# Scaling the hidden values in PSUM, eight plain products in two of twelve groups, and a longer spacing of the weight narrowing, in a fused attention, mixture and feed-forward kernel

## The chip, the cores and the metric

One Trainium2 chip, one core of it. The metric is the device time of one execution in microseconds (us). Three runs of the kernel before gave a median of 903.39 us (902.93 to 903.54).

## What is computed

Three stages in a row, all in fp32 (the last stage's weights arrive as 64-bit floats and are narrowed to fp32 on the chip):

```python
q_pool = q.reshape(B, H, S // 2, 2, D).mean(axis=3)          # B 2, H 8, S 1152, D 64
attn = softmax(q_pool @ k.T / sqrt(D)); x = attn @ v          # x: 1152 tokens x 512
p = domain_probs / domain_probs.sum(-1)                       # 1152 x 4
for e in range(4):                                            # w1: 4 x 512 x 1024
    out += p[:, e:e+1] * (maximum(x @ w1[e], 0) @ w2[e])
h = out @ w_in                                                # 512 x 2048
y = where(h > 0, h, exp(minimum(h, 0)) - 1) @ w_out           # 2048 x 512
```

## The kernel before

**Stages and groups.** `attention_then_moe_then_elu_ffn` runs attention first (16 heads), then twelve groups that are built alike: groups 0 to 7 are the mixture (4 experts, two groups of 512 hidden columns each), groups 8 to 11 the feed-forward part (G1 is 8). All activations stay transposed: `acc` holds x, later the output, as 128 partitions x 4 chunks x 1152 tokens.

**One group.** A group has a first product (512 features to 512 hidden) and a second (512 hidden to 512 features). Every fp32 matrix is split into a high and a low part (`h` and `l` in the names), and a product is three matmuls: high by high, low by high, high by low (`product`, L1086). The first product is done with seven block products in place of eight (a Strassen scheme): `TURNS` lists the seven, each needs a sum or difference of quarters of the weights (`left_sum`, then `left_high` and `left_low`, tiles `sum`, `wh`, `wl`) and of quarters of x (`x_half_sum` and `x_half_high`, `x_half_low`, tiles `XH`, `XL`, `K`, `xh`, `xl`, `x4h`, `x4l`; the sums of x are written over `acc`). Each block product is done for two halves s of its 576 tokens; one such unit ("F") is 12 matmuls of 288 columns, so a group has 14 F units. Between units, partial sums leave PSUM: `keep` (ScalarE copies, tiles `u` and `c`) and `whole` (VectorE adds a PSUM bank and a kept sum, result in an SBUF tile `c`). The four hidden quarters are called 2, 3, 7 and 4. Each goes through `relu_high` (ScalarE, writes `hh`) and `hidden_low` (VectorE, writes `hl`); in groups 8 to 11 it is `elu_min`, `elu_exp`, `elu_whole`, `elu_high`, `hidden_low`, through an SBUF tile `t`.

**Second product.** Six units ("P") of 24 matmuls of 384 columns, on `hh`, `hl` and the split weights `w2h`, `w2l` (`second_high` on ScalarE, `second_low` on GpSimd). What comes out is multiplied by p on VectorE (`scaled_out`: tile `t` from a PSUM tile `p` and the broadcast probabilities `pb`) and added to `acc` on GpSimd (`add_out`).

**PSUM.** Four tiles `p` of two banks each are all there is; F chains and P units take them in turn, and a tile is free again when its reader is done.

**Narrowing.** The 64-bit weights come in 32 chunks. `narrow` turns each into fp32 with one ScalarE, six VectorE and one GpSimd instruction (tiles `d`, `nt`, `ne`) and stores it in DRAM, where groups 8 to 11 load it from.

**What sets the order.** The order on each engine is written by two planners: `order_of` for attention and `ffn_order` for the groups. They place operations by assumed durations, due times and free tiles (`ffn_ops`: each `op` has a dict of engines with a duration, its needs and a due time). The result is emitted in that order, and each engine's queue keeps it. `PACE` is the planned distance of narrowing chunks in ns: 11600 here.

Of the kernel before, what the change touches and what calls it, by code (L numbers as in the profile page):

```python
# [133 lines left out]
def attention_ops(NH, KC):  # L134
# [99 lines left out]
def order_of(ops):  # L234
# [38 lines left out]
    while ready:  # L273
# [43 lines left out]
def ffn_ops(NG, G1, turns):  # L317

    ops, begin, plan, now = {}, {}, [], 0
    blocks = [[0, 1, 2] if g == 0 else [2, 1, 0] for g in range(NG)]  # L320
    for g in range(NG):
        for i in turns[g]:
            for s in (0, 1):
                begin["F", g, i, s] = now
                plan.append(("F", g, i, s))
                now += 1592
        for b in blocks[g]:
            for m in (0, 1):
                parts = (0, 1) if (g, b, m) == (NG - 1, 0, 1) else (2,)
                for z in parts:  # L330
                    begin["P", g, b, m, z] = now
                    plan.append(("P", g, b, m, z))
                    now += 4162 if z == 2 else 2081
    begin["end"] = now
    slots = {("F", g, i, s): 0 for g in range(NG) for i in turns[g] for s in (0, 1)}

    def op(key, on, need, due, after=0, lag=0, takes=None, gives=()):
        ops[key] = dict(on=on, need=need, due=due, after=after, lag=lag, takes=takes, gives=list(gives))
# [3 lines left out]

    prev = None
    for key in plan:
        g = key[1]
        if key[0] == "F":
            i, s = key[2:]
            need = [prev, ("o", g, i), ("Y", g, i, s)]
            need += {6: [("u", g, 1, s)], 7: [("u", g, 6, s)], 4: [("u", g, 7, s)], 3: [("c", g, 7, s)]}.get(i, [])
            last = {1: 4, 5: 3, 2: 2}.get(i)  # L350
            op(key, dict(PE=1592), need, begin[key], takes=last and "ps")
# [8 lines left out]
    conv = [(g, i) for g in range(NG) for i in turns[g]]  # L360
    for n, (g, i) in enumerate(conv):
        if n < 4:
            continue
        free = [("F", *conv[n - 4], 1)]
        due = begin["F", g, i, 0]
        need = [("W", g)]
        fast = g >= G1
        if i not in (1, 2, 4):
            old = [("o", g - 1, 5), ("o", g - 1, 7)]
            if turns[g].index(5) < turns[g].index(7):  # L370
                before = {5: old, 6: [("s", g, 5), ("o", g - 1, 3)], 7: [("o", g, 5), ("s", g, 6)], 3: [("o", g, 6)]}[i]
            else:
                before = {7: old, 6: [("s", g, 7), ("o", g - 1, 3)], 5: [("o", g, 7), ("s", g, 6)], 3: [("o", g, 6)]}[i]
            op(("s", g, i), dict(POOL=1300, DVE=690) if fast else dict(POOL=1300), need + before, due - 2400)
            need = [("s", g, i)]
        op(("h", g, i), dict(ACT=610), need, due - 1700, takes="w")
        op(("o", g, i), dict(POOL=1300, DVE=690) if fast else dict(POOL=1300), [("h", g, i)], due - 1300)
# [884 lines left out]
```

## Time and profile before

| what | value |
|---|---|
| median of 3 runs | 903.39 us |
| the profiled execution | 903.64 us, its span 901.9 us |
| PE (TensorE) busy | 836.9 us |
| DVE (VectorE) busy | 678.9 us |
| POOL (GpSimd) busy | 471.8 us |
| ACT (ScalarE) busy | 414.9 us |
| mean granted TensorE clock | 0.972 of full speed |

The profile is one execution taken by the hardware profiler. The first instruction is at 0, the last ends at 901.9; some 1.7 us of the run's time lie around that. PE is TensorE's matmuls, PEld its weight loads, SP the queue that issues most DMAs. Each view gives times from the span's start, so a stage can be cut out by the moments when its first and last matmuls start.

### The profile page before, as it was taken

The page shows a single profiled execution, that of the slowest core. Times are in us where ns is not written, and L with a number is a line of the kernel's source. Part 1 is how long each engine was busy: PE and PEld are TensorE (multiplying, and loading weights), DVE is VectorE, ACT ScalarE, POOL GpSimd, SP SyncE. Part 2 cuts the span into 40 slices and gives each one's busy share as a digit, 9 for nine tenths or more (in the row PEclk, how much of TensorE's full clock was granted, in tenths as well). Part 3 has the DMA queues.
Part 4 walks back from the last instruction along what each step waited for, and adds up shares of the span by engine and source line. Part 5 has one row for each costly group of instructions (what it writes and reads, how often), then busy time and mean ns, then how long its engine had stood idle before and what let it go on. Part 6 is the DMA issues. An engine that isn't in the chain of part 4 may idle for free.

```text
span 901.9 us, 14280 instructions
## 1 busy us (share of the span) xinstructions
PE 836.9 (93%) x5470; PEld 772.2 (86%) x5470; DVE 678.9 (75%) x891; ACT 414.9 (46%) x853; POOL 471.8 (52%) x410
## 2 busy tenths in 40 slices
PE   8998999899997999898999999899994789999998
PEld 7776778677776999898998998899993779999998
DVE  8775678577678668787868877787889984858583
ACT  7775668577755142422514142342514444425250
POOL 4351342273346268858776877859768551404000
PEclk9999999999998999999999999999997889999999
DMA  7997777864034241331424132232411402010002
GB/s 258 194 211 155 159 177 163 195 132 75 21 100 143 71 163 36 103 146 47 165 94 166 36 115 85 97 129 70 164 36 51 148 12 94 1 64 31 1 1 105
DMA packets 48356, 95.02 MB, mean 105 GB/s; under 512 B 14368, under 2 KB 26144, under 8 KB 45344
## 3 DMA queue, kind: packets, MB, share of 16 engines
q1 hardware_dynamic: 48144, 93.06, 36.8%
q10 hardware_dynamic: 144, 1.05, 0.3%
q8 instruction: 43, 0.70, 0.3%
q14 instruction: 25, 0.20, 0.1%
HBM read 64.37 MB, written 10.84 MB: 83 GB/s over the span
## 4 chain that ended last, share of the span: by engine, by line
PE 50%; DVE 24%; DMA 10%; POOL 6%; issue 5%; ACT 3%; SPq 1%; ACTq 0%; DVEq 0%; POOLq 0%
PE p L1090 31%; PE s L815 7%; PE s L900 6%; PE t L877 6%; DMA w<-nt 4%; DVE nt L1051 3%; DVE ne L1053 3%; DVE nt L1046 2%; DVE hl L1135 2%; DMA acc<-xo 2%; POOL acc L604 2%; POOL nt L1061 2%; DVE c L604 2%; DVE nt L1042 2%; DVE t L1151 1%
## 5 line engine op out<-in xcount | busy, mean ns | idle before, releaser
L1090 PE MATMUL p<-hh,w2h 128*128 128x384 f32 x576 | 193.9, 337 | 4.9 <-ACT hh L601 3.3
L1090 PE MATMUL p<-hl,w2h 128*128 128x384 f32 x576 | 194.4, 338 | 2.6 <-DVE hl L604 1.2
L1090 PE MATMUL p<-hh,w2l 128*128 128x384 f32 x576 | 193.6, 336 | 0.0
L826 DVE TENSOR_REDUCE st<-s 128x1 f32<-128x512 f32 (+1 forms) x144 | 105.6, 750 | 22.4 <-PE s L815 19.0
L815 PE MATMUL s<-K,Q 128*128 128x320 f32 (+1 forms) x480 | 112.1, 361 | 8.5 <-DVE xo L601 3.8
L1090 PEld LDWEIGHTS p<-hh,w2h 128*128 128x128 f32 x576 | 108.9, 189 | 5.7 <-ACT hh L601 4.0
L1090 PEld LDWEIGHTS p<-hl,w2h 128*128 128x128 f32 x576 | 108.9, 189 | 4.6 <-DVE hl L604 2.2
L832 ACT ACTIVATE e<-s,st 128x512 f32<-128x512 f32 (+1 forms) x144 | 106.3, 746 | 6.1 <-DVE st L826 3.8
L1090 PEld LDWEIGHTS p<-hh,w2l 128*128 128x128 f32 x576 | 109.0, 189 | 0.0
L877 PE MATMUL t<-ident,e 128*128 128x128 f32 x648 | 95.5, 279 | 2.6 <-ACT e L832 1.7
L877 PEld LDWEIGHTS t<-ident,e 128*128 128x128 f32 x648 | 76.5, 142 | 23.6 <-issue 7.6
L604 POOL TENSOR_TENSOR acc<-acc,t 128x768 f32<-128x768 f32 x42 | 86.2, 2055 | 19.9 <-DVE t L604 19.9
L815 PEld LDWEIGHTS s<-K,Q 128*128 128x128 f32 x480 | 75.4, 193 | 15.8 <-DVE xo L601 4.2
L1090 PE MATMUL p<-K,wh 128*128 128x288 f32 x384 | 79.7, 301 | 8.9 <-DVE c L604 6.7
L604 POOL TENSOR_TENSOR st<-st,st 128x5 f32<-128x5 f32 (+2 forms) x80 | 19.2, 249 | 119.6 <-DVE st L848 82.4
L1035 ACT ACTIVATE nt<-d 128x512 f32<-128x512 f32 x32 | 21.5, 670 | 125.2 <-DMA w<-nt 113.4
L900 PE MATMUL s<-pt,v 128*64 128x288 f32 x576 | 76.7, 412 | 0.0
L1061 POOL TENSOR_TENSOR nt<-nt,ne 128x512 f32<-128x512 f32 x32 | 44.5, 1390 | 60.3 <-DVE ne L1057 60.3
L601 ACT COPY pt<-t 128x384 f32<-128x384 f32 (+1 forms) x125 | 55.2, 456 | 42.7 <-PE t L877 38.7
L604 POOL TENSOR_TENSOR wl<-w,wh 128x512 fp32r<-128x512 f32 x35 | 52.9, 1523 | 40.3 <-ACT wh L601 40.3
L601 DVE COPY pt<-t 128x384 f32<-128x384 f32 (+1 forms) x115 | 56.2, 501 | 22.2 <-PE t L877 18.3
L1090 PE MATMUL p<-xh,wl 128*128 128x288 f32 x192 | 60.0, 313 | 13.5 <-POOL wl L604 13.5
(115 smaller groups left out, 1979.8 us busy)
## 6 DMA issues: line engine op xcount, KB each, us to landing
d<-in_va SPq DMA_DIRECT2D x16, 512.0 KB, 4.0
w<-nt SPq DMA_DIRECT2D x32, 256.0 KB, 3.4
d<-in_vb SPq DMA_DIRECT2D x16, 512.0 KB, 4.1
w<-w SPq DMA_DIRECT2D x8, 1024.0 KB, 4.8
Q<-q SPq DMA_DIRECT2D x28, 288.0 KB, 6.1
w<-in_wa SPq DMA_DIRECT2D x7, 1024.0 KB, 7.0
w<-in_wb SPq DMA_DIRECT2D x7, 1024.0 KB, 4.9
v<-in_v SPq DMA_DIRECT2D x16, 288.0 KB, 5.9
```

The costliest lines, as they stand in the source:

```text
L601: (nc.scalar.copy if e == "ACT" else engines[e].tensor_copy)(out, a)
L604: engines[e].tensor_tensor(out=out, in0=a, in1=b, op=op)
L815: nc.tensor.matmul(out=t[:, j], lhsT=q[:, o : o + P], rhs=ks[p % 2][:, y, c : c + PARTS[z][1]], start=k == x == 0, stop=2 * k + x == last,)
L826: nc.vector.tensor_reduce(out=nm[b, z], in_=s_t[b, z], axis=AX.XY, op=ALU.max, negate=True)
L832: nc.scalar.activation(et[b % NP][:, part(z)].rearrange("p (j k) -> p j k", j=PARTS[z][0]), s_t.pop((b, z)), AF.Exp, bias=nm.pop((b, z)), ...
L877: nc.tensor.transpose(t[:, c * P : c * P + P], et[b % NP][:, (3 * u + c) * P : (3 * u + c + 1) * P], ident)
L900: nc.tensor.matmul(out=tb[i, h][64 * z : 64 * z + 64, :HQ], lhsT=raws[i, "v"][:, c, :], rhs=pt[i % 2][:, c, half(z)], start=c == cs[0], st ...
L1035: nc.scalar.activation(nt, hi.bitcast(F32), AF.Abs)
L1051: nc.vector.tensor_tensor(out=ti, in0=ti, in1=ei, op=ALU.bitwise_xor)
L1053: nc.vector.tensor_scalar(out=ei, in0=ti, scalar1=0xFF800000, scalar2=None, op0=ALU.bitwise_and)
L1061: nc.gpsimd.tensor_tensor(out=nt, in0=nt, in1=ne, op=ALU.add)
L1090: nc.tensor.matmul(out=out, lhsT=w[a][:, c, m * P : m * P + P], rhs=x[b][:, c], start=new and c == a + b == 0, stop=c == cs - 1 and a == 1 ...
```

## The change

- **p multiplied into h.** In groups 0 to 7 the hidden value is made by one VectorE instruction, max(h, 0) times p, in place in PSUM (`hidden`); ScalarE then only copies it into `hh`. `scaled_out`, its tile `t` and the 42 GpSimd additions into `acc` are gone: `add_out` on VectorE adds a PSUM tile straight to `acc`.
- **Sums written back in PSUM.** `whole` writes its sum over the PSUM tile it read (quarter 7 takes a tile of its own), no longer into an SBUF tile `c`. So `hl` is made from a PSUM tile. In groups 8 to 11 only quarter 3 stays in PSUM to the end.
- **Two first products plain.** Groups 0 and 8 do the ordinary eight block products (16 F units) on unsummed quarters (`CLASSIC`, `plan_of`). The sums of x that the seven-product groups need are made during groups 0 and 8, behind their units, and no longer before. The first results of groups 0 and 8 are copied into `acc` by ScalarE when all splits of x are done.
- **Narrowing over eleven groups.** `PACE` goes from 11600 to 15500.
- **x scaled into a part of the result's space.** `x_scaled` writes its sum into a corner of `acc` that is not yet in use, for the first 14 heads.
- **The planner.** GpSimd and those VectorE operations that work in SBUF alone get a flag `port` and are planned one after the other; the last group of the mixture does its P units with m outermost; ScalarE may do `elu_min` as Relu of -h.

```diff
...
-LATE_X = 15500
-PACE = 11600
+LATE_X = 9500
+PACE = 15500
...
+CLASSIC = {(1, 1): 2, (2, 2): 2, (8, 1): 4, (4, 2): 4, (1, 8): 3, (2, 3): 3, (8, 8): 7, (4, 3): 7}
+
+
+def plan_of(NG, G1):
+    units, orders, lefts = [], [], []
+    for g in range(NG):
+        if g in (0, G1):
+            late = [(l, 1, s) for l in (1, 8) for s in (0, 1)] + [(l, 2, s) for l in (2, 4) for s in (0, 1)]
+            soon = [x for a, b in ((1, 2), (8, 4)) for s in (0, 1) for x in ((a, 8, s), (b, 3, s))]
+            units.append(late + soon if g else soon + late)
+            lefts.append((1, 8, 2, 4) if g else (1, 2, 8, 4))
+        else:
+            lefts.append((1, 2, 6, 7, 4, 5, 3))
+            units.append([(i, i, s) for i in lefts[g] for s in (0, 1)])
+        orders.append([(b, m) for b in ((2, 1, 0) if g else (0, 1, 2)) for m in (0, 1)])
+    orders[G1 - 1] = [(b, m) for m in (0, 1) for b in (2, 1, 0)]
+    return units, orders, lefts
...
+                old = [("Y", g, i, s) for i in range(1, 9) for s in (0, 1)] if g in (0, G1) else [("t", g - 1, b, m, 2)]
+                on = dict(ACT=820) if g in (0, G1) else dict(DVE=955 if z == 2 else 560)
+                op(("t", *k), on, [key] + old, after + 6000 - 5000 * (g == NG - 1), gives=[("ps", key)])
...
+            if x["port"]:
+                t = max(t, port)
...
+        def x_whole(i):
+            return acc[:, DC - 1, T - HQ * (1 + i % 2) :][:, :HQ] if i < NH - 2 else xo[i % 3][:, 0]
+
         def x_scaled(e, i):
             x = xo[i % 3]
             tt(e, x, x, fb[i % 2].rearrange("p (q z) -> p z q", z=2), ALU.mult)
-            tt(e, x[:, 0], x[:, 0], x[:, 1], ALU.add)
+            tt(e, x_whole(i), x[:, 0], x[:, 1], ALU.add)
...
     def whole(e, g, q, s, n=None):
...
+        a = psum(2 if q == 2 else 5, s)
+        b = kept[7, s] if q == 7 else part_sums[{2: 1, 3: 6}[q]][:, s]
+        if q == 7 and n is not None:
+            kept[q, s] = banks[n][:, :, :SB]
+        elif q != 7:
+            kept[q, s] = a
+        tt(e, kept[q, s], a, b, ALU.add)
...
+    def hidden(e, g, q, s):
+
+        _, _, c, n = hid(g, q, s)
+        if g < G1:
+            p = pb[:, n].unsqueeze(1).to_broadcast([P, 2, SB])
+            nc.vector.scalar_tensor_tensor(out=c, in0=c, scalar=0.0, in1=p, op0=ALU.max, op1=ALU.mult)
...
-    def scaled_out(e, g, b, m, z, n=None):
+    def add_out(e, g, b, m, z):
         o, s = out_of(b, m, z)
...
-            tmp[b, m, z] = ts[n]
-            tt(e, ts[n], s, p, ALU.mult)
-
-    def add_out(e, g, b, m, z):
-        o, _ = out_of(b, m, z)
-        tt(e, o, o, tmp[b, m, z], ALU.add)
+            tt(e, o, s, o, ALU.add)
...
```

How the order moves, at three places. In the rows, `hl` and `hh` are the split hidden values, `p_...` PSUM tiles, `c_...` and `u_...` SBUF sums, `ne`, `nt`, `d` the narrowing.

VectorE, late in the F units of a middle group of the mixture, before:

```order
L604 TENSOR_TENSOR c_2702<-p_2697,c_2702 128x576
L604 TENSOR_TENSOR c_2701<-p_2699,c_2701 128x576
L1135 SCALAR_TENSOR_TENSOR hl<-c_2702,hh 128x2x288
L1135 SCALAR_TENSOR_TENSOR hl<-c_2701,hh 128x2x288
L604 TENSOR_TENSOR c_2703<-p_2697,u_2696 128x576
L604 TENSOR_TENSOR c_2702<-p_2699,u_2696 128x576
L1135 SCALAR_TENSOR_TENSOR hl<-c_2703,hh 128x2x288
L1037 TENSOR_SCALAR ne<-d 128x512
```

VectorE at the same place of a middle group, now:

```order
L1151 SCALAR_TENSOR_TENSOR p_2686<-p_2686,pb 128x2x288
L611 TENSOR_TENSOR hl<-p_2686,hh 128x2x288
L1151 SCALAR_TENSOR_TENSOR p_2687<-p_2687,pb 128x2x288
L611 TENSOR_TENSOR p_2686<-p_2684,c_2689 128x2x288
L611 TENSOR_TENSOR hl<-p_2687,hh 128x2x288
L1151 SCALAR_TENSOR_TENSOR p_2686<-p_2686,pb 128x2x288
L611 TENSOR_TENSOR p_2687<-p_2685,c_2690 128x2x288
L1151 SCALAR_TENSOR_TENSOR p_2687<-p_2687,pb 128x2x288
L611 TENSOR_TENSOR hl<-p_2686,hh 128x2x288
```

The multiplication by p stands between a sum and its split, and the sum of quarter 7 (`p_2686<-p_2684,c_2689`) takes the tile that quarter 4 has just left, so it stands behind quarter 4's `hl`.

GpSimd, around the start of a group of the mixture (the last `wl` is that of the third block product), before:

```order
L604 TENSOR_TENSOR acc<-acc,t_2704 128x2x384
L1061 TENSOR_TENSOR nt<-nt,ne 128x512
L604 TENSOR_TENSOR acc<-acc,t_2705 128x2x384
L604 TENSOR_TENSOR w2l<-w,w2h 128x512
L604 TENSOR_TENSOR acc<-acc,t_2706 128x2x384
L604 TENSOR_TENSOR w2l<-w,w2h 128x512
L604 TENSOR_TENSOR wl_86<-sum_74,wh_85 128x512
```

GpSimd at the same place, now:

```order
L611 TENSOR_TENSOR sum_73<-w 128x512
L1063 TENSOR_TENSOR nt<-nt,ne 128x512 x2
L611 TENSOR_TENSOR w2l<-w,w2h 128x512 x3
L611 TENSOR_TENSOR wl_84<-sum_74,wh_83 128x512
L611 TENSOR_TENSOR w2l<-w,w2h 128x512
```

The additions into `acc` are gone, and three `w2l` stand ahead of the `wl` of the third block product where two stood, mixed with additions.

VectorE, in the F units of group 8, before (`XL`, `K` are splits of x, `acc<-acc` sums of x):

```order
L604 TENSOR_TENSOR XL<-acc,XH 128x2x288 x2
L1037 TENSOR_SCALAR ne<-d 128x512
L1042 TENSOR_SCALAR nt<-nt 128x512
L604 TENSOR_TENSOR acc<-acc 128x2x288
L1046 TENSOR_SCALAR nt<-nt 128x512
L604 TENSOR_TENSOR K_75<-acc,K_75 128x2x288
L1051 TENSOR_TENSOR nt<-nt,ne 128x512
L604 TENSOR_TENSOR K_75<-acc,K_75 128x2x288
L1053 TENSOR_SCALAR ne<-nt 128x512
L604 TENSOR_TENSOR c_2703<-p_2700,u_2695 128x576
```

VectorE in group 8, now:

```order
L1039 TENSOR_SCALAR ne<-d 128x512
L1044 TENSOR_SCALAR nt<-nt 128x512
L611 TENSOR_TENSOR acc<-acc 128x2x288
L1048 TENSOR_SCALAR nt<-nt 128x512
L611 TENSOR_TENSOR xl<-acc,xh 128x2x288
L1053 TENSOR_TENSOR nt<-nt,ne 128x512
L611 TENSOR_TENSOR xl<-acc,xh 128x2x288
L1055 TENSOR_SCALAR ne<-nt 128x512
L1153 SCALAR_TENSOR_TENSOR p_2685<-t_2657,p_2685 128x2x288
L1059 SCALAR_TENSOR_TENSOR ne<-d,ne 128x512
L1153 SCALAR_TENSOR_TENSOR p_2686<-t_2657,p_2686 128x2x288
L611 TENSOR_TENSOR hl<-p_2685,hh 128x2x288
```

Before, the first `c` of the group, which a PSUM tile waits for, stands behind the sums and splits of x; now the sums and splits ahead of the first hidden value are those for group 9, and the splits that group 8's own units read stand further up.

## Rows read from the trace of the kernel before

**Rows 1.** The page's head: the span, and busy time and share of each engine.

```profile
span 901.9 us, 14280 instructions
PE 836.9 (93%) x5470; PEld 772.2 (86%) x5470; DVE 678.9 (75%) x891; ACT 414.9 (46%) x853; POOL 471.8 (52%) x410
```

**Rows 2.** Stretches: length, busy us of PE, PEld, DVE, ACT, POOL, then granted clock.

```profile
259.43:316.84 57.41, 50.69 (x312) 49.89 (x313) 41.35 (x50) 21.57 (x36) 24.21 (x18) 0.94 0.37 120
316.84:364.09 47.25, 47.25 (x314) 47.25 (x313) 35.03 (x38) 15.27 (x26) 35.22 (x24) 1.00 0.34 110
364.09:675.45 311.36, 293.38 (x1874) 289.79 (x1873) 253.01 (x259) 104.77 (x177) 234.49 (x147) 0.98 0.30 103
675.45:753.63 78.18, 56.17 (x314) 53.75 (x313) 62.73 (x67) 31.00 (x51) 44.86 (x27) 0.85 0.18 61
753.63:898.35 144.72, 142.98 (x937) 141.61 (x936) 99.98 (x133) 56.58 (x93) 26.04 (x16) 1.00 0.12 45
```

**Rows 3.** PE in order of time: first F, first P matmul of group 1, first of 2.

```profile
316.84 0.29 PE L1090 MATMUL p<-XH,wh 128*128 128x288 f32 x1
...
339.11 0.33 PE L1090 MATMUL p<-hh,w2h 128*128 128x384 f32 x1
...
364.09 0.29 PE L1090 MATMUL p<-XH,wh 128*128 128x288 f32 x1
```

**Rows 4.** PE's waits from 259.43 on: us in total, times, longest.

```profile
PE p L1090 <- DVE c L604: 20.1, 5, 11.8
PE p L1090 <- POOL wl L604: 13.5, 6, 3.0
```

**Rows 5.** PE in order of time: waits (in brackets) of groups 7 and 8.

```profile
632.86 0.60 PE L1090 MATMUL p<-xh,wl 128*128 128x288 f32 x1 [2.58 <-POOL wl L604]
...
695.67 0.58 PE L1090 MATMUL p<-XH,wh 128*128 128x288 f32 x1 [11.81 <-DVE c L604]
```

**Rows 6.** POOL in order of time, the start of group 7 (it starts at 623.50).

```profile
627.71 2.02 POOL L604 TENSOR_TENSOR acc<-acc,t 128x768 f32<-128x768 f32 x1
629.69 1.45 POOL L604 TENSOR_TENSOR w2l<-w,w2h 128x512 fp32r<-128x512 f32 x1
631.11 1.70 POOL L604 TENSOR_TENSOR wl<-sum,wh 128x512 fp32r<-128x512 f32 x1
```

**Rows 7.** Groups by shape, 320 to 645 us: count, busy us, mean ns of one.

```profile
L604 POOL TENSOR_TENSOR acc<-acc,t 128x768 f32<-128x768 f32 x36 | 73.5, 2044 | 15.2 <-DVE t L604 15.2
L1135 DVE SCALAR_TENSOR_TENSOR hl<-c,hh 128x576 fp32r<-128x576 f32 x38 | 51.4, 1362 | 6.4 <-ACT hh L1130 5.9
...
L604 DVE TENSOR_TENSOR t<-p,pb 128x768 f32<-128x768 f32 x36 | 33.8, 947 | 6.4 <-PE p L1090 6.4
...
L1051 DVE TENSOR_TENSOR nt<-nt,ne 128x512 uint32<-128x512 uint32 x24 | 31.7, 1322 | 0.5
...
L1046 DVE TENSOR_SCALAR nt<-nt 128x512 uint32<-128x512 uint32 x24 | 27.4, 1142 | 0.5
...
L1053 DVE TENSOR_SCALAR ne<-nt 128x512 uint32<-128x512 uint32 x24 | 25.1, 1045 | 0.4
...
L1037 DVE TENSOR_SCALAR ne<-d 128x512 uint32<-128x512 uint32 x24 | 22.7, 947 | 20.3 <-DMA d<-in_va 10.3 <-DMA d<-in_vb 9.9
L1057 DVE SCALAR_TENSOR_TENSOR ne<-d,ne 128x512 f32<-128x512 uint32 x23 | 19.8, 863 | 0.5
...
L1042 DVE TENSOR_SCALAR nt<-nt 128x512 f32<-128x512 f32 x24 | 19.4, 810 | 23.9 <-ACT nt L1035 23.8
L604 DVE TENSOR_TENSOR c<-p,u 128x576 f32<-128x576 f32 x26 | 19.3, 748 | 4.7 <-PE p L1090 4.7
...
L1135 DVE SCALAR_TENSOR_TENSOR hl<-p,hh 128x576 fp32r<-128x576 f32 x13 | 9.8, 754 | 3.0 <-ACT hh L1130 3.0
```

**Rows 8.** DVE in order of time, F units of group 8.

```profile
684.67 2.03 DVE L1037 TENSOR_SCALAR ne<-d 128x512 uint32<-128x512 uint32 x1
...
694.78 0.74 DVE L604 TENSOR_TENSOR c<-p,u 128x576 f32<-128x576 f32 x1
```

More of the change, by code (lines that the diff above doesn't have):

```diff
@@ L285, in order_of @@
         free[e] = start + of(o)[e]
-        end[o] = free[e] + LATE.get(o[0], LAG[e])
+        end[o] = free[e] + (SOON if e == "SP" and o[1:] >= (12,) else LATE.get(o[0], LAG[e]))
         x, bank = takes(o), None
@@ L319, in ffn_ops, with chain_of @@
+def chain_of(g, G1, l, r):
+    if g in (0, G1):
+        return CLASSIC[l, r], r in (1, 8)
+    return {6: 1, 7: 1, 4: 1, 3: 5}.get(l, l), l in (1, 2, 5)
+def ffn_ops(NG, G1):
     ops, begin, plan, now = {}, {}, [], 0
-    blocks = [[0, 1, 2] if g == 0 else [2, 1, 0] for g in range(NG)]
+    units, orders, lefts = plan_of(NG, G1)
     for g in range(NG):
[L322 to L338, printed above, removed]
+        for x in units[g]:
+            begin["F", g, *x] = now
+            plan.append(("F", g, *x))
+            now += 1592
+        for b, m in orders[g]:
+            for z in (0, 1) if (g, b, m) == (NG - 1, 0, 1) else (2,):
+                begin["P", g, b, m, z] = now
+                plan.append(("P", g, b, m, z))
+                now += 4162 if z == 2 else 2081
@@ L340, in unit, with op, first @@
+    def op(key, on, need, due, after=0, lag=0, takes=None, gives=(), port=False):
+        ops[key] = dict(on=on, need=need, due=due, after=after, lag=lag, takes=takes, gives=list(gives), port=port)
     def unit(g, b, m):
         return [("P", g, b, m, z) for z in (0, 1, 2) if ("P", g, b, m, z) in begin]
+    def first(g, l=None, r=None, s=None):
+        return [("F", g, *x) for x in units[g] if l in (None, x[0]) and r in (None, x[1]) and s in (None, x[2])]
+    both = dict(POOL=1430, DVE=755)
@@ L346, in ffn_ops @@
         if key[0] == "F":
[L347 to L351, printed above, removed]
+            l, r, s = key[2:]
+            need = [prev, ("o", g, l), ("Y", g, r, s)]
+            if g not in (0, G1):
+                need += {6: [("u", g, 1, s)], 7: [("u", g, 6, s)], 4: [("u", g, 7, s)], 3: [("c", g, 7, s)]}.get(l, [])
+            op(key, dict(PE=1592), need, begin[key], takes="ps" if chain_of(g, G1, l, r)[1] else None)
         else:
@@ L358, in ffn_ops @@
         prev = key
[L360 to L377, printed above, removed]
@@ L387, in ffn_ops @@
-        end = [k for b in blocks[g - 1] for m in (0, 1) for k in unit(g - 1, b, m)] if g else []
-        first = begin["P", g, blocks[g][0], 0, 2]
+            op(("W", g), dict(SP=350), late + stored(0), begin[first(g)[0]] - 18000, lag=8500)
+        op(("Z", g), dict(SP=350) if g else dict(ACT=100), [("L", g - 1, c) for c in range(4)] + stored(1), begin[first(g)[-1]] - 15000, lag=8500 if g else 7000, after=0 if g else 6500)
+        end = [k for x in orders[g - 1] for k in unit(g - 1, *x)] if g else []
@@ L427, in ffn_ops @@
+        for b, m in orders[g]:
             for key in unit(g, b, m):
```

325 lines of the change are left out of this document (147 added, 178 removed).

## The prediction, made before the changed kernel was run

> **What bounds the kernel now.** I read the page's head first [rows 1]: TensorE (PE) is busy for 837 of 901.9 us, so only what makes PE wait, or adds work to it, can move the time. Next I cut the span at PE's first matmuls of the groups and asked for busy times by stretch [rows 2]. Group 1 is the clean case: 47.25 us, PE busy all of it, at full clock. Its F units take 22.27 us (14 of 1.59 us) and its P units 24.98 us [rows 3]. Every other stretch is held against that price. Attention ends, and group 0 starts, at 259.43. Then:
>
> - group 0, the first row of [rows 2]: 57.41 us, 10.2 us over 47.25;
> - groups 2 to 7: 311.36 us, 27.9 over six times 47.25, or 4.6 each;
> - group 8: 78.18 us, 30.9 over;
> - groups 9 to 11: 144.72 us, 3.0 over.
>
> That is 72 us of lost PE time, and twelve groups at 47.25 are 567 us. After 898.35 come 3.55 us of last addition and store. 259.43 + 567.0 + 72.0 + 3.55 = 902.0, the span.
>
> The list of PE's waits says whom PE waits for [rows 4]: VectorE's sums `c` (20 us) and GpSimd's low parts `wl` (13.5 us). These two are 33.6 of the 72 us. [...] Group 7 shows the ratio: its one large wait is 2.58 us [rows 5], the group loses about 4.6, so a wait costs some 1.8 times its length.
>
> Two places matter. In a group of the mixture the wait is for the `wl` of the third block product. GpSimd's own order shows why [rows 6]: an addition into `acc` (2.02 us) and a `w2l` (1.45) stand right ahead of it, with another addition and `w2l` before those. In group 8, PE stands for 11.8 us [rows 5] until a `c` that takes VectorE 0.74 us, at 694.78 [rows 8], which queued behind sums and splits of x and narrowing.
>
> Engine load by group says whether there is room. In groups 2 to 7, VectorE is busy for 253 of 311 us (81%) and GpSimd for 234 (75%) [rows 2].
>
> **The change, part by part.**
>
> *Plain products.* Two groups get 16 F units for 14, so PE does 4 units of 1.59 us more [rows 3]: **+6.4 us**, all on the path.
>
> *Group 0.* The sums of x leave the units' way. The eight units on token half 0 come first and need nothing from the last heads. I take 2 us of loss in place of 10.2; ends 0 and 10 (nothing better than now). What could be late is the first hidden value's `hl`, which frees a PSUM tile and is due eight units (12.7 us) in; it stands behind the last heads' scaling and two sums of x on VectorE. A group's results may go to `acc` only when all splits of x are done; four P units (16.7 us) fit before a tile must be back.
>
> *Groups 1 to 7.* GpSimd loses six additions of 2.04 us per group [rows 7] and, by the slower narrowing, about one `nt`. Today 234.5 / 6 = 39.1 us per group; left are some 26 of 47 us, so 55%. Ahead of the third product's `wl` now stand three `w2l` (the order shows it): four GpSimd instructions of 1.45 us [rows 6] are 5.8, behind a ScalarE cast that starts with the group. PE needs that `wl` after four F units and two matmuls, 6.6 us, which leaves 0.8 us for the cast. So it is just in time, and the 2.6 us wait goes.
> VectorE per group, now: 6 sums at 0.75, 8 `hl` of which 6 read two SBUF tiles at 1.36 and 2 a PSUM tile at 0.75, 6 scalings at 0.95 [rows 7], 19.9 us. After: 6 sums, 8 multiplications by p, 8 `hl`, all on PSUM tiles at 0.75, and 6 additions into `acc` at 0.95: 22.2 us. A narrowing chunk is 6.1 us on VectorE (the six means in [rows 7]); there come 32 / 11 = 2.9 per group, 17.9 us, where today one comes every 13.5 us (24 in 325 us), 3.8 per group of 51.9 us. Sum after: 40 of 47 us, 85%. VectorE is no worse off than now by load, but it is now the fuller engine. I take 0.7 us of loss per group, **5 us** for seven; ends 0 and 27.9 (as now).
> Two costs in this part are not in the trace. No VectorE instruction writes PSUM there, and none multiplies in place. The nearest rows are those that read PSUM, 0.748 and 0.754 us, then `t<-p,pb` at 0.947 for 768 columns with the same broadcast; the dearest of that size is `hl<-c,hh` at 1.362 [rows 7]. I take 0.75, since both sides of the nearest row use a PSUM operand; at 1.36 the 64 multiplications cost VectorE 4.9 us more per group and it would be 95% full. A gain over 0.75 has no row for it.
>
> [...]
>
> *Group 8.* Its units read unsummed quarters, whose splits are due one at a time while the mixture's last P units run (m outermost gives the first half early). The 30.9 us loss should mostly go. What is late next: the first four chains take all four PSUM tiles, and the ninth unit waits for the first hidden value, a chain of five instructions on two engines that has 4.7 us (three units). In VectorE's order a narrowing of five instructions and three sums and splits stand right before it. By [rows 7] and [rows 8] such instructions take 0.8 to 2.0 us where GpSimd runs too, so 2 to 4 us late, once or twice, some of it paid 1.8 times. I take **7 us**; ends 2 and 20.
>
> *Groups 9 to 11.* Today's 32 chunks at 13.5 us take 433 us and end in group 8; at 15.5 us they take 496 and run through group 9. So group 9 looks more like the mixture. ScalarE takes part of `elu_min`. I take **5 us** in place of 3; ends 1 and 12.
>
> *Slower narrowing.* The last chunk is stored some 500 us after the groups start, near 760. By the sum below group 11, which needs it, starts after 800: zero, covered by some 40 us.
>
> *Attention and x scaled into `acc`.* The order changes only in the last 45 us or so, with fewer sums and splits there and the same PE work. PE hardly waits in that part now, so there is little to gain. I take zero, ends -1 and +3; if a late head's write were held up, the cover is the eight units (12.7 us) that need only token half 0.
>
> **Sum**, against the profiled execution (903.64 us, its span 901.9 and 1.7 around it): 259.4 + 567.0 + 6.4 + (2 + 5 + 7 + 5 = 19) + 3.55 = 855.4, with 1.7 around it **857 us**. The runs' median is 0.25 us under the profiled one, which changes nothing in the rounding.
>
> **Rivals.**
>
> 1. *The forecast*, 847 to 868: chance 0.60.
> 2. *Nearly no wait is left.* With 5 us of loss in all: 843. For it: the group of the clean case had VectorE at 35 of 47 us and GpSimd at 35, near what comes. Against it: PSUM tiles are now held through the multiplication and the split. 0.13.
> 3. *VectorE's queue is late in every group.* A narrowing instruction that meets GpSimd's work takes up to 2.03 us [rows 8], and one such ahead of a hand-over makes PE wait. At 2.03 times 1.8, 3.7 us for eleven groups, with group 0 as above and 5 more for group 8, give 47.7 us of loss: 886. For it: VectorE at 85%. Against it: hand-overs read PSUM at 0.75 us, and the narrowing mostly stands after them in the order. 0.20, spread over 869 to 893.
> 4. *PSUM runs out, and it gets slower.* A tile that was free after one sum is now held for sum, multiplication, ScalarE copy and split: four instructions at 0.75 (the ScalarE copy taken alike), 3.0 us, and with two narrowing instructions of 1.2 us [rows 7] in between 5.4. If PE waits for that once in each of twelve groups, 65 us, with group 8's 7 us beside it, the time is 259.4 + 567 + 6.4 + 65 + 7 + 5.3 = 910. It decides from 5.6 us per group on, since the edits otherwise give back 72 - 6.4. Against it: in the order the quarter's split comes before the sum that takes its tile, with three units (4.8 us) between. 0.06.
> 5. *The change does not do what it says*, because what PE waited for was hidden by something as late behind it: 903. Since the two waits sit at different places with different causes, 0.01.
>
> **How the numbers follow.** The likeliest is the forecast, 857. 844 to 880 holds its whole case, most of the second and the lower half of the third: 0.60 + 0.09 + 0.11. A difference under 0.2% (1.8 us) can't be told from no change here. Faster is cases 1 to 3, 0.93; slower is case 4, 0.06; no change 0.01.
>
> **What would show it.** Right: F and P stages of 47.3 us in groups 2 to 7, with waits for `wl` under 1 us; granted clock 1.00 in most of them; 50.4 us and a few more for groups 0 and 8; `hl<-p,hh` and the multiplication at 0.75 us each; GpSimd near 26 us per group. The forecast is wrong if the multiplication into PSUM takes over 1 us, if PE waits for `hl` at the fifth block product or at the first P unit in each group (case 3, or 4 above 5 us), or if group 8 still takes over 65 us.

## The result, and the profile after

The changed kernel takes **835.14 us** (median of four runs, 834.55 to 835.81), the kernel before 903.46. The ratio is 0.9235, with a 95% interval of 0.9208 to 0.9262. The forecast was 857 with a range of 844 to 880: the direction was right, the gain was 68 us where 46 were forecast, and the time lies below the range.

The page's head of the changed kernel, against [rows 1]:

```profile
span 834.0 us, 14379 instructions
...
PE 819.6 (98%) x5518; PEld 762.5 (91%) x5518; DVE 589.3 (71%) x922; ACT 428.1 (51%) x883; POOL 322.4 (39%) x344
```

Its stretches, cut at PE's first matmuls of group 0, 1, 2, 8 and 9 and at the end of its last one, with the columns of [rows 2]:

```profile
248.25:306.15 57.90, 52.83 (x336) 52.13 (x337) 39.13 (x51) 21.13 (x34) 28.85 (x20) 0.97 0.36 112
306.15:353.46 47.31, 47.31 (x313) 47.26 (x313) 32.12 (x46) 18.58 (x32) 25.62 (x20) 1.00 0.33 111
353.46:637.78 284.32, 283.78 (x1873) 283.46 (x1873) 204.69 (x285) 102.61 (x174) 138.11 (x106) 1.00 0.31 103
637.78:688.33 50.55, 50.55 (x337) 50.46 (x337) 38.82 (x63) 29.90 (x49) 13.13 (x8) 1.00 0.29 94
688.33:830.51 142.18, 142.18 (x937) 141.62 (x936) 91.18 (x134) 72.04 (x124) 19.75 (x15) 1.00 0.19 64
```

Groups 2 to 7 take 284.32 us, 0.8 over six times 47.25; group 8 takes 50.55, 0.1 over 47.25 and two F units. Only group 0 still loses more than 1 us, 7.5 over its 50.43 (47.25 and two units of 1.59). And group 0 starts at 248.25, where it started at 259.43.

PE's waits, in the columns of [rows 4]; `c` and `wl` are gone from the list:

```profile
PE p L1092 <- DVE hl L611: 5.6, 4, 2.0
PE t L882 <- ACT e L837: 2.0, 5, 0.8
```

VectorE's groups by shape in groups 2 to 7, against [rows 7]:

```profile
L1151 DVE SCALAR_TENSOR_TENSOR p<-p,pb 128x576 f32<-128x576 f32 x48 | 36.0, 760 | 4.9 <-PE p L1092 4.3
L611 DVE TENSOR_TENSOR hl<-p,hh 128x576 fp32r<-128x576 f32 x48 | 35.7, 750 | 6.9 <-ACT hh L608 6.7
L611 DVE TENSOR_TENSOR acc<-p,acc 128x768 f32<-128x768 f32 x36 | 34.4, 955 | 48.6 <-PE p L1092 48.6
...
L1039 DVE TENSOR_SCALAR ne<-d 128x512 uint32<-128x512 uint32 x18 | 17.5, 971 | 3.5 <-POOL w2l L611 1.8 <-DMA d<-in_va 0.9 <-DMA d<-in_vb 0.7
L1053 DVE TENSOR_TENSOR nt<-nt,ne 128x512 uint32<-128x512 uint32 x18 | 13.3, 742 | 0.4
L1055 DVE TENSOR_SCALAR ne<-nt 128x512 uint32<-128x512 uint32 x18 | 12.6, 698 | 0.6
L1059 DVE SCALAR_TENSOR_TENSOR ne<-d,ne 128x512 f32<-128x512 uint32 x18 | 12.4, 688 | 0.4
L1044 DVE TENSOR_SCALAR nt<-nt 128x512 f32<-128x512 f32 x18 | 9.7, 539 | 0.0
...
L1048 DVE TENSOR_SCALAR nt<-nt 128x512 uint32<-128x512 uint32 x18 | 7.7, 426 | 0.5
```

The multiplication into PSUM takes 0.76 us and `hl` 0.75, as taken. The six narrowing means add up to 4.1 us a chunk, where [rows 7] gave 6.1.

The difference to the forecast, by stage: attention -11.2, group 0 +5.5, groups 1 to 7 -4.1, group 8 -6.9, groups 9 to 11 -4.6; together -21.3 of the 21.4 us between 855.4 and the span of 834.0.

### The profile page after: what moved, and what is told of

Read it like the earlier page. It is cut to its first block, busy times and chain, and to the rows that moved or that the text cites. A ratio compares the mean times of both kernels' runs of the same rounds, so it can differ in the third digit from the quotient of the medians.

```text
span 834.0 us, 14379 instructions
## 1 busy us (share of the span) xinstructions
PE 819.6 (98%) x5518; PEld 762.5 (91%) x5518; DVE 589.3 (71%) x922; ACT 428.1 (51%) x883; POOL 322.4 (39%) x344
## 4 chain that ended last, share of the span: by engine, by line
PE 92%; DVE 3%; DMA 2%; ACT 2%; issue 0%; POOL 0%; SPq 0%; DVEq 0%
PE p L1092 66%; PE s L820 9%; PE s L905 8%; PE t L882 8%; DMA fb<-dr 1%; ACT e L837 1%; DMA q<-in 1%; ACT pt L608 1%; DVE hl L611 0%; DMA dr<-st 0%; DVE p L1151 0%; DVE st L831 0%; DVE K L611 0%; POOL st L611 0%; DVE acc L611 0%
## 5 line engine op out<-in xcount | busy, mean ns | idle before, releaser
L611 DVE TENSOR_TENSOR acc<-p,acc 128x768 f32<-128x768 f32 (+1 forms) x61 | 57.5, 942 | 89.5 <-PE p L1092 89.4
L1063 POOL TENSOR_TENSOR nt<-nt,ne 128x512 f32<-128x512 f32 x32 | 42.7, 1336 | 193.0 <-DVE ne L1059 193.0
L820 PE MATMUL s<-K,Q 128*128 128x320 f32 (+1 forms) x480 | 109.2, 355 | 0.7 <-ACT e L837 0.7
L882 PE MATMUL t<-ident,e 128*128 128x128 f32 x648 | 93.7, 276 | 2.7 <-ACT e L837 2.0
L1092 PE MATMUL p<-K,wh 128*128 128x288 f32 x448 | 90.7, 296 | 0.0
L608 ACT CAST hh<-p 128x576 fp32r<-128x576 f32 x78 | 50.0, 641 | 69.8 <-DVE p L1151 66.9
L1092 PEld LDWEIGHTS p<-K,wh 128*128 128x128 f32 x448 | 72.3, 189 | 0.3 <-DVE p L611 0.2
L1092 PE MATMUL p<-XH,wh 128*128 128x288 f32 x224 | 66.8, 298 | 5.6 <-DVE hl L611 5.1
L1092 PE MATMUL p<-XH,wl 128*128 128x288 f32 x224 | 66.4, 296 | 0.0
```

The costliest lines, as they stand in the source:

```text
L608: (nc.scalar.copy if e == "ACT" else engines[e].tensor_copy)(out, a)
L611: engines[e].tensor_tensor(out=out, in0=a, in1=b, op=op)
L820: nc.tensor.matmul(out=t[:, j], lhsT=q[:, o : o + P], rhs=ks[p % 2][:, y, c : c + PARTS[z][1]], start=k == x == 0, stop=2 * k + x == last,)
L882: nc.tensor.transpose(t[:, c * P : c * P + P], et[b % NP][:, (3 * u + c) * P : (3 * u + c + 1) * P], ident)
L1063: nc.gpsimd.tensor_tensor(out=nt, in0=nt, in1=ne, op=ALU.add)
L1092: nc.tensor.matmul(out=out, lhsT=w[a][:, c, m * P : m * P + P], rhs=x[b][:, c], start=new and c == a + b == 0, stop=c == cs - 1 and a == 1 ...
```

## The experiments

All runs in one table. "Start" is PE's first matmul of group 0. A loss is the length of the stretch (cut as above, at PE's first matmuls) less 47.25 us per group, and less 3.18 more in a group with plain products. Start and losses are those of one profiled execution; the median is of four (e2: ten). For e6 and e10 that execution took the most of the four (876.24 and 855.44 us), so their losses are at the high end.

| run | start | loss, group 0 | groups 1 to 7 | group 8 | median us |
|---|---|---|---|---|---|
| before | 259.43 | 10.2 | 27.9 | 30.9 | 903.5 |
| changed | 248.25 | 7.5 | 0.9 | 0.1 | 835.1 |
| e1 xo as before | 257.34 | 6.5 | 0.9 | 0.1 | 843.6 |
| e2 before, xo edit alone | 249.05 | 11.7 | 30.8 | 31.0 | 894.9 |
| e3 narrowing at 11600 | 248.28 | 6.4 | 4.3 | 0.6 | 840.0 |
| e4 later load | 248.39 | 1.7 | 1.9 | 0.1 | 831.5 |
| e5 p at the output | 249.22 | 1.6 | 0.5 | 8.4 | 839.3 |
| e6 sums in SBUF | 248.46 | 8.2 | 40.1 | 0.7 | 872.8 |
| e7 group 8 with seven | 248.75 | 6.5 | 0.8 | 8.0 | 841.9 |
| e8 as e6, own tiles | 249.13 | 6.6 | 15.1 | 0.1 | 851.8 |
| e9 no rule | 248.89 | 13.6 | 1.4 | 1.4 | 843.9 |
| e10 as e5, no rule | 249.42 | 6.7 | 6.5 | 13.8 | 853.2 |

### Attention: one edit undone, and the same edit alone

The theory (A) came from reading the kernel before once more, over attention. Its list of waits, for all engines from 20 to 250 us, has these lines:

```profile
ACT xo L601 <- DMA acc<-xo: 5.4, 1, 5.4
DVE xo L601 <- DMA acc<-xo: 5.1, 1, 5.1
...
PE s L815 <- DVE xo L601: 3.8, 1, 3.8
...
PE s L815 <- ACT xo L601: 3.2, 2, 2.7
```

The copy of a new head into a tile xo waits for the transfer of an older head's sum out of that tile, and PE, whose PSUM tile that copy frees, waits behind it. e1, on the changed kernel:

```diff
         def x_whole(i):
-            return acc[:, DC - 1, T - HQ * (1 + i % 2) :][:, :HQ] if i < NH - 2 else xo[i % 3][:, 0]
+            return xo[i % 3][:, 0]
```

> The changed kernel with one edit undone: the sum of scaled x goes back into its own tile xo, and the store into acc reads it from there; every engine's order stays as it is. Theory A (in attention the kernel before lost time because a tile xo could not be written again until its transfer into acc had landed, and PE stood for it, with the half clock behind): group 0 starts near 259 in place of 248.25, PE shows waits for xo of 2 to 4 us again, and the time is 843 to 848 us. Rival B (the 11 us came from the fewer sums and splits late in attention): group 0 starts at 248 to 250 and the time is within 2 us of 835.

e2 puts the same edit, and no other, into the kernel before:

```diff
+        def x_whole(i):
+            return acc[:, DC - 1, T - HQ * (1 + i % 2) :][:, :HQ] if i < NH - 2 else xo[i % 3][:, 0]
...
-            tt(e, x[:, 0], x[:, 0], x[:, 1], ALU.add)
+            tt(e, x_whole(i), x[:, 0], x[:, 1], ALU.add)
...
-                    out=acc[r : r + D, h // 2, c], in_=xo[i % 3][D * z : D * z + D, 0]
+                    out=acc[r : r + D, h // 2, c], in_=x_whole(i)[D * z : D * z + D]
```

> The kernel before with that one edit alone: the sum of scaled x goes into the unused corner of acc for the first 14 heads. Theory A: the waits of PE for xo go, group 0 starts 8 to 11 us earlier (248 to 251), and the time is 892 to 896 us. Rival B: group 0 starts at 258 to 260 and the time is within 2 us of 903.

e1 took 843.57 us (842.66 to 843.95), 8.4 more than the changed kernel, and group 0 started at 257.34. The waits are back, in the list of e1 for the same stretch:

```profile
ACT xo L608 <- DMA acc<-xo: 6.6, 2, 4.5
DVE xo L608 <- DMA acc<-xo: 6.1, 1, 6.1
...
PE s L820 <- DVE xo L608: 4.8, 1, 4.8
...
PE s L820 <- ACT xo L608: 1.8, 1, 1.8
```

e2 took 894.86, 8.6 less than the kernel before (ratio 0.9908, interval 0.9878 to 0.9938), and its group 0 started at 249.05. Theory A holds in both kernels. Of 11.2 us in attention the edit gives 9 to 10; 1 to 2 us (249.05 to 248.25, 259.43 to 257.34) are left to the rest of the change and were not taken apart. The waits alone are 7.0 us in the kernel before; the rest goes with a lower granted clock behind them (0.50 from 73.20 to 76.40 us and from 168.80 to 172.00, where waits of 3.8 and 2.7 us had ended at 73.21 and 167.83). Two stretches of that kernel (60 to 100 and 140 to 180 us), with the columns of [rows 2]:

```profile
60.00:100.00 40.00, 36.00 (x251) 27.97 (x247) 26.69 (x49) 26.88 (x70) 14.36 (x24) 0.96 0.79 159
140.00:180.00 40.00, 37.11 (x259) 28.98 (x259) 26.76 (x47) 26.98 (x70) 11.71 (x21) 0.96 0.78 176
```

The same two of the changed kernel:

```profile
60.00:100.00 40.00, 39.76 (x290) 30.18 (x285) 28.54 (x54) 28.67 (x74) 17.83 (x30) 1.00 0.92 183
...
140.00:180.00 40.00, 39.76 (x290) 31.33 (x288) 29.89 (x55) 30.70 (x81) 14.99 (x29) 1.00 0.79 183
```

### Group 0: a load that stands in the way of another

In the changed kernel VectorE stands idle before the last head's scaling, with hidden values queued behind it. VectorE in order of time (start, length, idle time before in brackets):

```profile
258.54 0.76 DVE L611 TENSOR_TENSOR xo<-xo,fb 128x576 f32<-128x576 f32 x1 [11.34 <-DMA fb<-dr]
...
260.38 1.42 DVE L1151 SCALAR_TENSOR_TENSOR p<-p,pb 128x576 f32<-128x576 f32 x2
```

The transfers that were issued at the same time, 236 to 266 us (size, us to landing):

```profile
w<-in_wb ACTq DMA_DIRECT2D x1, 1024.0 KB, 9.5
...
fb<-dr SPq DMA_DIRECT2D x4, 144.0 KB, 6.2
pb<-pr ACTq DMA_DIRECT2D x1, 576.0 KB, 6.1
```

e4 has ScalarE issue the first of these only after its first cast of a hidden value:

```diff
-        op(("Z", g), dict(SP=350) if g else dict(ACT=100), [("L", g - 1, c) for c in range(4)] + stored(1),
+        op(("Z", g), dict(SP=350) if g else dict(ACT=100), [("L", g - 1, c) for c in range(4)] + stored(1) + [("x", 0, 3, 0)] * (g == 0),
```

> The changed kernel with one transfer later: in group 0 ScalarE issues the 1 MB load of the second product's weights after its first cast of a hidden value, so that it no longer runs beside the last heads' factors fb. Theory E (VectorE's queue stood 11.3 us for fb because that load and pb shared the engines of the DMA with it, and PE's waits in group 0 follow from that): fb lands 3 to 6 us earlier, the 5 us of PE waits and the half clock in group 0 go for the most part, and the time is 828 to 831 us. Rival F (fb takes as long without that load, or PE's waits have another cause): the time is within 1.5 us of 835; if the weights of the second product then come late, it is longer than 836.

It took 831.48 us (831.08 to 833.66). VectorE's line is now

```profile
255.83 0.76 DVE L611 TENSOR_TENSOR xo<-xo,fb 128x576 f32<-128x576 f32 x1 [8.88 <-DMA fb<-dr]
```

2.7 us earlier, a little less than theory E's 3 to 6 us, and the time is half a us above its 828 to 831. Of the 8.88 us that VectorE still stands there, 3.2 pass before the loads of fb are issued at all (at 250.14, when the store of `dr` that they read has landed). PE's waits in group 0 go from 5.1 to 1.0 us and the half clock goes from its stretch (in the changed kernel the granted clock was 0.50 from 272.50 to 274.50 us and 0.95 over group 0's F units; over these it is 1.00 now). Group 1 gives 1.1 us of that back: its F units take 23.39 us in place of 22.35. The pair was timed again, side by side:

> The changed kernel as it is, timed again beside the version with the later load: 835 us within 1 us, with group 0 at 57.9 us as in its first profile.

> The version with the later load of the second product's weights in group 0, timed again beside the changed kernel: 831.5 us within 1 us and 3 to 4.5 us below the changed kernel's median, with group 0 at 52 us. If the earlier difference was chance, the two medians are within 1.5 us of each other.

835.35 (834.97 to 837.31) against 831.83 (830.96 to 833.03), 3.5 us apart. The version with the later load is the fastest one here, and faster than both kernels. pb still lands beside fb; moving it was not tried.

### Groups 1 to 7: p in h, the sums in PSUM, the planner's rule, the spacing

The forecast's reason for the vanished `wl` wait was that GpSimd loses six additions per group. e5 gives them back, by the code of the kernel before for that part, and leaves the sums in PSUM (to make room, the tiles t grow and one of three tiles c goes):

```diff
-            p = pb[:, n].unsqueeze(1).to_broadcast([P, 2, SB])
-            nc.vector.scalar_tensor_tensor(out=c, in0=c, scalar=0.0, in1=p, op0=ALU.max, op1=ALU.mult)
+            nc.scalar.activation(hid(g, q, s)[0], c, AF.Relu)
...
+            tmp[b, m, z] = ts[n]
+            tt(e, ts[n], s, p, ALU.mult)
+
+    def add_out(e, g, b, m, z):
+        o, _ = out_of(b, m, z)
+        tt(e, o, o, tmp[b, m, z], ALU.add)
```

> The changed kernel with p back at the output of the mixture: ScalarE casts max(h, 0) into hh, VectorE makes hl from the PSUM tile, the outputs are scaled by p into tiles t on VectorE and added to acc on GpSimd (six additions per group again); the sums stay in PSUM. Theory G (moving p into h is what took the stall out of groups 1 to 7, because GpSimd then has six additions of some 2 us less ahead of the weights' low parts): GpSimd goes from some 24 to some 36 us per group, PE waits for wl or w2l in most groups again, 2 to 5 us per group lost, time 850 to 868 us. Rival H (the sums in PSUM, whose hl takes 0.75 in place of 1.36 us, are what did it; GpSimd has room for the additions): groups 2 to 7 stay within 0.5 us of 47.25, time 834 to 840 us.

Theory G fell. GpSimd was busy 246 of 331 us in groups 1 to 7 (74%; 75% in the kernel before), and PE lost 0.5 us in seven groups. The time, 839.26 us (838.95 to 840.41), is 4.1 above the changed kernel for another reason: group 8 loses 8.4 us, with PE waiting for `hl` (2.1 us) and `hh` (2.8) and the granted clock at 0.94. The sums and splits of x there need group 7's additions, which GpSimd now makes. The trace shows the chain behind the first of the two waits: an addition, ScalarE's cast behind it, VectorE's split behind that.

```profile
636.21 2.24 POOL L617 TENSOR_TENSOR acc<-acc,t 128x768 f32<-128x768 f32 x1 [3.16 <-DVE t L617]
638.48 1.25 ACT L614 CAST K<-acc 128x576 fp32r<-128x576 f32 x2 [4.22 <-POOL acc L617]
639.19 1.14 DVE L617 TENSOR_TENSOR K<-acc,K 128x576 fp32r<-128x576 f32 x1 [2.45 <-ACT K L614]
```

Two more splits of x and two `w2l` follow on VectorE, and the `hl` that PE waits for ends at 647.4. Group 0 is 5.9 us shorter; there the order put a cast ahead of the load of e4, which was issued at 252.77 in place of 248.61, and VectorE stood 8.1 us for fb.

What the additions do cost is VectorE's narrowing. Two of e5's lines for groups 2 to 7, against 539 and 688 ns above:

```profile
L1065 DVE SCALAR_TENSOR_TENSOR ne<-d,ne 128x512 f32<-128x512 uint32 x18 | 23.6, 1314 | 0.2
L1050 DVE TENSOR_SCALAR nt<-nt 128x512 f32<-128x512 f32 x18 | 23.1, 1283 | 6.0 <-ACT nt L1043 6.0
```

A chunk takes 6.4 us there, 4.1 without the additions. PE did not pay for that.

e6 keeps p in h, and writes the sums of quarters 2 and 3 of groups 1 to 7 into SBUF tiles c:

```diff
-            kept[q, s] = a
+            kept[q, s] = a if n is None else cs[n]
```

> The changed kernel with the sums of quarters 2 and 3 of groups 1 to 7 written to SBUF tiles c again, and multiplied by p and split there; p stays in h. Theory H: four multiplications and four splits per group then read and write SBUF beside GpSimd's work, at 0.9 to 1.4 us in place of 0.75, VectorE gets 2 to 5 us more per group and PE waits for hl: 2 to 4 us per group, time 849 to 863 us. Theory G, and a reading by which copying out of PSUM first is no loss: groups 1 to 7 stay within 0.7 us of 47.25, time 834 to 840 us.

872.82 us (870.23 to 876.24), more than theory H gave. But the wait was not the one it named:

```profile
PE p L1099 <- ACT c L1123: 19.8, 7, 3.9
PE p L1099 <- DVE p L618: 5.7, 4, 2.7
```

PE waits for ScalarE's copy of quarter 7 (L1123), which takes a tile c. e8 gives these copies the tiles t, which are idle in these groups:

```diff
-            kept[7, s] = cs[n]
+            kept[7, s] = (ts if g < G1 else cs)[n]
```

> The run with sums in SBUF again (quarters 2 and 3 of groups 1 to 7), but the copies of quarter 7 get tiles t of their own, so that a tile c is no longer what ScalarE's copy waits for. Theory K (that run lost its 5 us per group to the three tiles c, which a quarter now holds through sum, multiplication, cast and split, and not to slower instructions): the waits of PE for c go, groups 1 to 7 lose at most 1 us each, time 835 to 843 us. Theory H (instructions on SBUF beside GpSimd are the cost): PE waits for hl or for the sums of quarter 7 instead, 2 to 5 us per group, time 849 to 870 us.

851.8 us (848.83 to 855.24): 21 of e6's 38 us were the tiles, and 15.1 us of loss in groups 1 to 7 remain with the sums in SBUF, as theory H said. PE waits there for `hl` (4.9 us) and for quarter 7's sum (5.0). VectorE's lines in e8, groups 2 to 7:

```profile
L1158 DVE SCALAR_TENSOR_TENSOR c<-c,pb 128x576 f32<-128x576 f32 x24 | 31.0, 1303 | 0.1
L618 DVE TENSOR_TENSOR hl<-c,hh 128x576 fp32r<-128x576 f32 x24 | 22.3, 937 | 0.1
L1158 DVE SCALAR_TENSOR_TENSOR p<-p,pb 128x576 f32<-128x576 f32 x24 | 17.9, 758 | 4.4 <-PE p L1099 4.4
...
L618 DVE TENSOR_TENSOR hl<-p,hh 128x576 fp32r<-128x576 f32 x24 | 17.5, 748 | 1.7 <-ACT hh L615 1.6
```

The same multiplication takes 1303 ns on average on an SBUF tile and 758 on a PSUM tile, the same split 937 and 748. The single multiplications spread further than these means (shortest, median and longest in ns; first and last start):

```profile
L1158 DVE SCALAR_TENSOR_TENSOR c<-c,pb x24: 744/1412/1861, 366.0 to 632.1; 128x576 f32<-128x576 f32 x24
L1158 DVE SCALAR_TENSOR_TENSOR p<-p,pb x24: 751/756/767, 371.1 to 625.9; 128x576 f32<-128x576 f32 x24
```

Ten of those on SBUF ran with no GpSimd instruction beside them, or with one for about a quarter of their time at most. They took 744 to 755 ns, no longer than on PSUM. Of the other fourteen, twelve took 1772 to 1861 ns (the last two 759 and 1053). So an SBUF tile is not slower by itself here (744 to 755 ns), and all twelve long multiplications ran beside GpSimd. On PSUM all 24 took 751 to 767 ns; in groups 2 to 7 of the changed kernel this multiplication took 755 to 767 ns the 13 times that GpSimd was idle, and 748 to 767 the 35 times that it ran.

VectorE is busy for 75% of groups 1 to 7 in e8 (260 of 346 us) and 71% in the changed kernel (237 of 332), so on average it has room in both. But ahead of each of PE's five waits for `hl` in groups 1 to 7 of e8, VectorE works without a pause, and two SBUF multiplications of 1.77 to 1.85 us each stand in that row of work: there it is the length of the hand-over. The waits for quarter 7's sum stand behind other hand-overs in VectorE's order. How much of the 15.1 us is owed to the other order that the planner gave e8, with these operations under its rule, was not taken apart.

e9 takes the planner's rule for GpSimd and SBUF operations out of the changed kernel, e10 out of e5:

```diff
-            if x["port"]:
-                t = max(t, port)
```

> The changed kernel without the planner's rule that GpSimd's operations and VectorE's operations in SBUF alone are planned one after the other; all else stays. Theory L (that rule keeps narrowing and GpSimd apart, so it holds the stall away): the narrowing instructions go from 4.1 back to about 6 us a chunk, VectorE to 85% in groups 3 to 7, PE waits for hl, time 843 to 858 us. Rival M (with sums in PSUM and the additions away from GpSimd there is room either way): groups 2 to 7 within 0.5 us of 47.25, time within 3 us of 835.

> The run with p back at the output, and without the planner's rule as well: what is left of the change in groups 1 to 7 is then the sums written in PSUM and the slower narrowing. Theory H (the sums in PSUM alone take the stall out): groups 2 to 7 within 0.7 us of 47.25, time 836 to 845 us. Theory L (the rule is what kept the additions away from the weights' low parts): PE waits for wl again, 2 to 5 us per group, time 850 to 870 us.

e9: 843.92 us (843.11 to 845.24). Groups 1 to 7 lose 1.4 us, so rival M was right on them and wrong on the time: the new order costs 6 us in group 0, where PE waits 8.8 us for `hl`. Theory L fell, though its range holds the time: a chunk takes 3.7 us, not 6, and PE waits for `hl` only once in groups 1 to 7, for 0.5 us. e10: 853.23 (849.67 to 855.44), and groups 1 to 7 lose 6.5 us, with waits for `wl` again (3.1 us, four times), so neither theory holds in full. Still, e10 has p at the output and no rule, as the kernel before, and loses 6.5 us where that lost 27.9: most of the gain in these groups comes with the sums in PSUM, the wider spacing and the rest of the new order, which were not parted here. With sums in PSUM, the rule is worth 6 us in these groups when GpSimd carries the additions, and 0.5 when it doesn't; p in h is worth 5 us without the rule and nothing with it (read from one execution of each run). Each covers for the other.

e3 was to show whether the room on VectorE is needed:

```diff
-PACE = 15500
+PACE = 11600
```

> The changed kernel with the planned distance of narrowing chunks back at 11600 ns. Theory C (the room on VectorE is what lets groups 1 to 7 run without loss): with about 3.9 chunks per group in place of 2.9, some 6 us more of VectorE work per group, VectorE stands near 85% in groups 3 to 7 and PE waits 1 to 3 us per group: 843 to 856 us. Rival D (the order and the PSUM hand-overs do it, the room is not needed): groups 2 to 7 stay within 0.5 us of 47.25 each and the time is within 3 us of 835.

840.02 us (838.98 to 841.21), but it didn't test that. The chunks came no closer, as GpSimd's last addition of a chunk shows in e3 (first and last start):

```profile
L1063 POOL TENSOR_TENSOR nt<-nt,ne x32: 1286/1292/1746, 277.9 to 739.2; 128x512 f32<-128x512 f32 x32
```

and in the changed kernel:

```profile
L1063 POOL TENSOR_TENSOR nt<-nt,ne x32: 1282/1294/1748, 279.0 to 749.0; 128x512 f32<-128x512 f32 x32
```

A chunk every 14.9 us against 15.2. The 4.9 us between the medians, 3.2 between the profiled spans, come from another order with the same work (a loss of 0.1 to 0.4 us a group in groups 1 to 6, and 2.4 us in group 7). The question of the spacing stays open.

### Group 8: plain or seven products

e7 gives group 8 its seven products back, with the sums of x ahead of the units (excerpt). It also changes where group 8's hidden values are made: in the changed kernel all four quarters of group 8 stay in PSUM to the end, and only from group 9 on is it quarter 3 alone; in e7 it is quarter 3 alone in group 8 too.

```diff
-    return g <= G1 or q == 3
+    return g < G1 or q == 3
...
-        if g in (0, G1):
+        if g == 0:
...
+                split(1, sums(1, 0), at[1])
+                total(1, [("Y", g, 1, z), *sums(0, 0)], at[6] - 4000)
+                split(5, [("T", g, 1, z)], at[6] - 4000)
```

> The changed kernel with group 8 on seven block products again: 14 units, in the order of the other groups, with the sums of x made before its units; group 0 stays plain. Theory I (the sums and splits of x in front of the units are what group 8 lost its 31 us to, and the two units more that the plain form costs buy that): PE stands 10 to 25 us in group 8, the time is 847 to 862 us. Rival J (the loss came from narrowing and SBUF sums in VectorE's queue, which the rest of the change has already taken out): group 8 loses at most 5 us and the time is 831 to 837 us.

841.9 us (839.79 to 843.14), between the two. Group 8 takes 55.29 us in place of 50.55: a loss of 8.0 us, where the kernel before lost 30.9. So 23 us of that loss went through the rest of the change, and the plain form, together with the quarters that stay in PSUM, is worth a net 4.7 us (8.0 less the 3.2 of two units more). The sums and splits of x, which theory I named, are not what PE's longest wait in group 8 of e7 shows. It is 2.9 us, for the ELU's last step on VectorE (L1167, in `hidden`), and what stands before that on VectorE is a sum and the low parts of weights, not of x:

```profile
655.59 1.69 DVE L625 TENSOR_TENSOR sum<-w,sum 128x512 f32<-128x512 f32 x1
657.20 2.50 DVE L625 TENSOR_TENSOR w2l<-w,w2h 128x512 fp32r<-128x512 f32 x2
659.62 1.41 DVE L1167 SCALAR_TENSOR_TENSOR t<-t,p 128x576 f32<-128x576 f32 x2
```

With plain products, p in h is worth 8.3 us in this group (e5). How the 23 us divide among the parts of the change was not separated.

## Why the prediction was wrong, and where it was right

**The step that failed** is the term "Attention and x scaled into `acc`": "PE hardly waits in that part now, so there is little to gain. I take zero, ends -1 and +3." The wait that the prediction left out is PE's for xo: 7 us there, in the list of waits that it read only from 259.43 on, and 9 to 10 us with the clock. The edit that the term names took it away (e1, e2). With -11.2 there the sum would have been 846 in place of 857; the other 10 us of the miss are the losses below.

**Groups 1 to 7, sized wrong, and for the wrong reason in part.** 5 us were taken, 0.9 measured. That the `wl` wait goes and that the multiplication takes 0.75 us was right; GpSimd came to 25.6 us in group 1 and 23.0 a group in 2 to 7, where some 26 were forecast. VectorE's load was wrong: 85% forecast, 72% measured in groups 2 to 7, since a chunk takes 4.1 us where GpSimd has no additions. And the six additions were not the cause that decides (e5): the sums in PSUM are needed (e8, with the order that came with it), and beside them it is enough either to take the additions away (e9) or to plan them apart (e5).

**PSUM or SBUF.** The rows were right to go by: 760 and 750 ns from PSUM, 1303 and 937 from SBUF (e8). But the 1362 ns of [rows 7], 1.36 us beside 0.75 from PSUM in the prediction's load of VectorE, are a mean over instructions with and without GpSimd beside them: eleven of these `hl` in groups 1 to 7, with GpSimd beside them for under 0.3 of their time, took 745 to 760 ns. Writing to SBUF first was the worse choice here: e8, which does so with two of the sums, is 17 us slower. Nor does the instruction take longer from PSUM: from 735 us on, `hl` in the changed kernel takes 752 ns from an SBUF tile and 751 from PSUM. And a row for a multiplication in place was there, against what the prediction says: `xo<-xo,fb` (128x576, at 263.44 in the kernel before) took 0.75 us, though in SBUF.

**Group 8**: 7 us taken, 0.1 measured; no chain was late. **Groups 9 to 11**: 5 taken, 0.4 measured. **Plain products**: 6.4 taken; group 8's 50.55 us is 47.25 and 3.3. **Narrowing**: the last chunk is added at 749, far before group 11 at 783; zero was right.

**Group 0**: 2 us taken, 7.5 measured. The place was named (the first `hl` behind the last heads' scaling), but not the transfer that scaling waits for, nor that the new order starts a 1 MB load beside it: at 248.61, just ahead of the last head's fb (248.85). In the kernel before that load starts at 263.00, after the last fb (261.56).

**The rivals.** In the groups it went as rival 2 said, nearly no wait; rivals 3 and 4 don't appear in the waits. Either part alone, the attention or the groups, would have left the time at 846 or 847, inside the range; it failed because rival 2's case came together with 11 us in the one term that no rival touched.

## What to carry to other kernels

Read the list of waits over the whole span before a stage is taken as untouched: an edit of one output tile was worth 9 us in a stage where PE waited for it only three times. Ask of a hand-over on VectorE where both its inputs lie; here the same instruction took 1.7 times as long on SBUF as on PSUM on average (1303 against 758 ns in e8), and some 2.4 times as long (1772 to 1861 ns) in twelve of the fourteen times that GpSimd ran beside it for more than about a quarter of its time, and that mattered though VectorE was busy for only 75%. When two edits both remove a stall, undo them one at a time and together, as neither shows its worth alone.

## What was not expected of the hardware

VectorE's narrowing instructions, which share no data with GpSimd's additions, took 4.1 us a chunk without these and 6.4 with them. One of them goes by two lengths: in groups 2 to 7 of the changed kernel `ne<-d` took 415 to 419 ns the eight times that GpSimd was idle, and 1.1 to 1.5 us the ten times that it ran. And the two fb loads of a head (144 KB each) were in use 4 us after the first was issued (242.00 to 245.95), while those of the last head took 9.7 us (248.85 to 258.54) beside 1.6 MB of other loads.
